# Mask operands in the rounded 32-bit type, and a list scheduler that knows kinds of matmul

## The chip, the core and the metric

The kernel runs on one core of a Trainium2 chip. The metric is device time in microseconds (us) for one execution. The core has five engines that run their own instruction streams: TensorE (PE; its weight loads are shown apart as PEld), VectorE (DVE), ScalarE (ACT), GpSimd (POOL) and SyncE (SP), which here only issues DMAs. They wait for one another through semaphores.

## The reference

Three stages follow one another. The sizes are 4 batches, 768 tokens, 8 heads of 48, model width 384, inner width 1024, 4 experts of 64.

```python
# stage 1, for every batch and head: a complex decay a_t, normalised, and a running state
S_re = ar*S_re - ai*S_im + k_t (x) v_t ;  S_im = ar*S_im + ai*S_re ;  y_t = q_t . S_re
# stage 2: a gated inner layer with a convolution of 3 taps along the tokens
h = relu(x @ w_in);  conv = sum_k conv_w[k] * shift(h, k);  x2 = (h * sigmoid(conv)) @ w_out
# stage 3: attention of 4 experts, each token mixing its best 2
scores = (x2 wq_e)(x2 wk_e)^T / 8, upper triangle set to -1e9;  a = softmax(scores)
out += [e in top 2] * w_e * (a @ (x2 wv_e)) @ wo_e
```

## The kernel before

All three stages are written as one list of operations (`S.op`), each with the engines that may run it, an estimated duration, the tiles it reads and writes, and a priority. `Sched.run` (lines 159 to 314) then plays a machine: at each moment it takes, for the engine that is free first, the ready operation with the smallest priority number that has buffer space, and `emit` writes the instructions in the order so found. The table `P` holds the offsets from which all priorities are made, and the buffer counts. So the order on every engine is fixed when the kernel is built; on the chip each engine works through its own list and waits only for data.

Buffers are arenas: F, R, Z, A to D in SBUF, and the 8 PSUM banks ("banks" in the rows). A matmul operand of the rounded 32-bit type (`F32R`) is made by a copy that rounds, followed by a subtraction that keeps the remainder; products are formed from the high and low parts. These matmuls are called rounded here: L743 and L781 (the two products of stage 2, nine matmuls each time), L901 (queries and keys), L851 (values), L1000 and L1001 (scores), L979 (output). Full 32-bit matmuls are L423, L571, L583, L591, L609, L613 (stage 1), L1024 and L947 (128x128 transposes by a matmul with the identity) and L958 (weights times values). L609, L613 and L958 use 48 or 64 of the 128 columns.

A score operation (`score`, L985) takes one block of 128 queries against n = 128 to 768 keys. It runs L1000 and L1001 over n columns, in two pieces where n is over 512, and then L1003, a matmul of `identb` (weights) with `maskb` (moving) that adds 1e30 above the diagonal of the last 128 columns. Both tiles are BF16. DVE then reduces the row minimum (L1009), ACT takes the exponential (L1011), and the transposes (L1024, in `turn`) turn the result, whose copies out of PSUM are L370 on ACT and L372 on DVE.

Idle gaps of PE in the first microseconds are filled with L627, matmuls of a zero tile.

Of the kernel before, what the change touches and what calls it, by code (L numbers as in the profile page):

```python
# [38 lines left out]
P = dict(tu=22.99, lag=1.78, tf=3.56, dn=29.40, pa=28.16, pf=31.65, pp=31.74, ps=19.16, pr=13.53, kn=9.56, pd=-10.31,  # L39
         py=-3.49, cw=7.07, cs=6.91, ne=3, sw=16.78, slack=0.33, hold=1.18, wl=0.23, bl=0.07, bc=0.37, hy=7.06,  # L40
         tb=28.68, xp=-21.85, jq=-1.43, jp=3.08, jv=-4.00, ja=-2.43, jf=16.61, jt=5.79, ju=0.10, jw=0.26, na=13, no=2,
         nt=6, ns=4, nx=7, nq=14, th=0.46, fr=0.20, nc=2, sd=1, ck=-587.37, up=61.76, big=0, a0=1, a1=4, u0=-0.59,
         u1=0.11, u2=3.11, u3=-0.41, u4=0.75, u5=1.55, u6=-0.26, u7=1.62, u8=0.57, u9=-4.01, u10=-7.57, u11=-0.52,
         v0=-0.57, v1=-0.88, v2=2.18, v3=0.15, v4=1.22, v5=1.18, v6=0.00, v7=-7.38, v8=-7.08, v9=-5.79, v10=3.04,
         v11=-7.00, b0=0.00, b1=-4.24, b2=-0.23, b3=7.87, b4=-0.60, b5=-0.53, b6=-3.32, b7=-1.95, b8=-2.61, c0=0.89,
         c1=-2.69, c2=1.81, c3=-0.52, pw=0.14, sp=1.00, jg=-4.92, pm=-1.39)
# [3 lines left out]
COLS = {"F": 19200, "R": 16420, "Z": 8264, "A": 2080, "B": 2080, "C": 2080, "D": 2080}  # L50
# [44 lines left out]
class Sched:  # L95
# [64 lines left out]
    def run(self):  # L160
        slack = P["slack"]
# [6 lines left out]
        dma, curtab, now, port, narrow = 0.0, None, 0.0, 0.0, 0.0  # L168
# [29 lines left out]
        while done < total:  # L198
# [492 lines left out]
def s2_ops(c):  # L691
# [42 lines left out]
    def ft(w, left, right, f, d, xh, xl, acc, group, nx, no):  # L734
# [62 lines left out]
def s3_ops(c):  # L797
# [21 lines left out]
    def batch(b):  # L819
# [22 lines left out]
        for i in range(NCB):  # L842
            ps = S.bank([128, NE + E], tag="pp", bufs=2)
            xh, xl = x2[i // 3]
            o = (i % 3) * 128

            def f(e, ps=ps, xh=xh, xl=xl, o=o):
                z = 0
                for x, a in ((xh, 0), (xl, 0), (xh, 1)):
# [5 lines left out]
            S.op({"PE": 9 * 0.12}, f, r=[xh, xl, wv[0], wv[1]], w=[ps], prio=pz)
# [35 lines left out]
    def project(n, wt, pr, tt, x, qk, pz):  # L891
# [80 lines left out]
    def final(b, i, o, y, d):  # L972
# [13 lines left out]
    def score(b, pr, i, r, d, qk, rs, at):  # L986
# [257 lines left out]
```

## Time and profile before

| what | us |
|---|---|
| median of 3 runs | 691.02 |
| lowest, highest | 687.9, 691.45 |
| the profiled execution, whole | 693.14 |
| its span in the profile | 691.3 |

The profiled execution took 1.8 us more than its span. Start and duration in a timeline row are us from the span's start. A matmul's shown duration reaches to its last result, so neighbours overlap; what a matmul costs PE is read from start to start. A run of n equal matmuls shows (n-1) spacings and one duration.

### The profile page before, as it was taken

What the parts mean: (1) busy time and instruction counts of PE and PEld (TensorE: products, weight loads), DVE (VectorE), ACT (ScalarE), POOL (GpSimd) and SP (SyncE); (2) the same over time, 40 slices, a digit from 0 to 9 for tenths busy, and PEclk for the clock granted to TensorE, in tenths of its full rate; (3) what the DMA queues carried; (4) which work ended last, traced back from release to release, by engine and by line L of the source; (5) the groups of instructions that cost most, each with busy time, mean ns of one, the idle gap of its engine ahead of it and who ended that gap; (6) DMA issues with size and microseconds to landing.
All of it is one profiled execution on the core that took longest, in us unless ns stands there. A gap on an engine that the chain in (4) does not pass through costs nothing.

```text
span 691.3 us, 13153 instructions
## 1 busy us (share of the span) xinstructions
PE 648.2 (94%) x4774; PEld 577.4 (84%) x4778; DVE 564.1 (82%) x1144; ACT 478.7 (69%) x1003; POOL 113.7 (16%) x157
## 2 busy tenths in 40 slices
PE   6789798899899999999999999989999999999995
PEld 3559587799899899999999999977878789788874
DVE  6998999989899999988759999687867676786661
ACT  7967886788898886875536756477667646766752
POOL 0723120240441411110011000011012100100101
PEclk9997999899999999999999999999999999999998
DMA  8665858746657366445132140020021001000102
GB/s 309 164 201 174 242 165 233 201 147 190 169 175 214 100 214 181 144 127 161 58 92 75 65 127 34 17 86 2 1 57 49 35 1 69 1 1 13 36 24 74
DMA packets 54603, 76.57 MB, mean 111 GB/s; under 512 B 5104, under 2 KB 45936, under 8 KB 54528
## 3 DMA queue, kind: packets, MB, share of 16 engines
q1 hardware_dynamic: 54240, 75.04, 35.7%
q8 instruction: 39, 0.64, 0.4%
q0 software_dynamic: 288, 0.59, 0.3%
q14 instruction: 36, 0.29, 0.1%
HBM read 42.51 MB, written 14.16 MB: 82 GB/s over the span
## 4 chain that ended last, share of the span: by engine, by line
PE 63%; DVE 19%; ACT 8%; DMA 5%; issue 3%; SPq 1%; DVEq 0%; ACTq 0%
PE banks L781 12%; PE banks L743 10%; PE banks L958 6%; PE banks L901 5%; PE banks L1024 4%; PE banks L571 4%; PE banks L851 3%; PE banks L979 3%; DVE arena_F L380 3%; PE banks L1000 3%; PE banks L423 3%; DVE arena_R L380 3%; PE banks L1001 2%; PE banks L591 2%; PE banks L609 2%
## 5 line engine op out<-in xcount | busy, mean ns | idle before, releaser
L781 PE MATMUL banks<-arena_R 128*128 128x384 f32 (+1 forms) x510 | 104.1, 343 | 0.0
L743 PE MATMUL banks<-arena_R 128*128 128x384 f32 (+1 forms) x472 | 101.6, 343 | 2.4 <-DVE arena_Z L596 0.9
L781 PEld LDWEIGHTS banks<-arena_R 128*128 128x128 f32 x510 | 88.3, 188 | 1.7 <-issue 1.3
L370 ACT ACTIVATE arena_F<-banks 128x384 f32<-128x384 f32 (+4 forms) x145 | 61.9, 453 | 39.8 <-PE banks L1024 18.7
L743 PEld LDWEIGHTS banks<-arena_R 128*128 128x128 f32 x472 | 82.3, 188 | 4.6 <-ACT arena_R L370 1.3
L765 DVE SCALAR_TENSOR_TENSOR arena_F<-arena_F 128x386 f32<-128x386 f32 (+1 forms) x128 | 77.5, 626 | 4.2 <-ACT arena_F L762 2.9
L370 ACT ACTIVATE arena_R<-arena_F 128x384 fp32r<-128x384 f32 (+2 forms) x82 | 43.0, 534 | 48.9 <-PE banks L781 20.5
L1011 ACT ACTIVATE arena_F<-banks,arena_F 128x128 f32<-128x128 f32 (+5 forms) x96 | 60.6, 640 | 14.4 <-DVE arena_F L1009 13.1
L380 DVE TENSOR_TENSOR arena_R<-arena_F,arena_R 128x384 fp32r<-128x384 f32 (+1 forms) x88 | 57.3, 668 | 14.6 <-PE banks L781 10.1
L380 POOL TENSOR_TENSOR arena_F<-arena_F 128x768 f32<-128x768 f32 x26 | 50.3, 1941 | 107.9 <-ACT arena_F L458 29.3
L1009 DVE TENSOR_REDUCE arena_F<-banks 128x1 f32<-128x128 f32 (+5 forms) x96 | 57.0, 617 | 8.3 <-PE banks L1003 7.6
L380 DVE TENSOR_TENSOR arena_F<-arena_F 128x768 f32<-128x768 f32 (+1 forms) x65 | 61.0, 954 | 0.5 <-ACT arena_F L437 0.3
L344 ACT ACT_TABLE_LOAD x40 | 51.3, 1283 | 1.4 <-PEq L1236 0.8
L1024 PE MATMUL banks<-ident,arena_F 128*128 128x128 f32 x336 | 49.0, 276 | 0.6 <-ACT arena_F L370 0.4
L754 ACT ACTIVATE arena_F<-banks 128x384 f32<-128x384 f32 (+1 forms) x64 | 31.0, 486 | 25.5 <-PE banks L743 21.7
L1000 PE MATMUL banks<-arena_R 128*128 128x384 f32 (+4 forms) x112 | 41.7, 375 | 1.6 <-ACT arena_F L1011 1.6
L372 DVE COPY arena_F<-banks 128x512 f32<-128x512 f32 (+4 forms) x75 | 37.6, 516 | 6.7 <-PE banks L1024 2.8
L958 PE MATMUL banks<-arena_F 128*64 128x384 f32 (+2 forms) x288 | 41.4, 430 | 0.0
L609 PE MATMUL banks<-arena_Z 128*64 128x128 f32 x384 | 37.5, 283 | 3.9 <-DVE arena_Z L573 3.0
L1024 PEld LDWEIGHTS banks<-ident,arena_F 128*128 128x128 f32 x336 | 37.1, 141 | 3.2 <-ACT arena_F L370 1.3
L768 DVE SCALAR_TENSOR_TENSOR arena_F<-arena_F 128x384 f32<-128x384 f32 (+1 forms) x64 | 36.4, 588 | 3.6 <-ACT arena_F L767 3.2
L573 DVE TENSOR_TENSOR arena_Z<-banks,tri 128x512 f32<-128x512 f32 x48 | 31.9, 681 | 5.9 <-PE banks L571 5.2
(242 smaller groups left out, 1480.0 us busy)
## 6 DMA issues: line engine op xcount, KB each, us to landing
arena_F<-x_scr SPq DMA_DIRECT2D x12, 576.0 KB, 4.5
arena_Z<-v SPq DMA_DIRECT2D x12, 512.0 KB, 5.0
arena_C<-arena_F SPq DMA_DIRECT2D x36, 129.0 KB, 2.4
arena_F<-q SPq DMA_DIRECT2D x12, 384.0 KB, 3.8
arena_F<-k SPq DMA_DIRECT2D x12, 384.0 KB, 4.7
arena_B<-arena_F SPq DMA_DIRECT2D x36, 128.0 KB, 2.4
x_scr<-arena_Z SPq DMA_DIRECT2D x24, 192.0 KB, 3.5
out<-arena_F SPq DMA_DIRECT2D x24, 192.0 KB, 1.9
```

The source lines that it names most:

```text
L344: nc.scalar.preload_act_table_set(TABS[o.tab])
L370: self.A.activation(out(), in_(), AF.Copy)
L380: self.E[e].tensor_tensor(out(), a(), b(), op=self.OPS[op])
L609: PE.matmul(ps[64 * i:64 * i + 64, g_, :], v[:, ci, 2 * g_ + i, :], sm[g_ // 2][:, 2 * (g_ % 2) + i, :], start=True, stop=(cc == 0))
L743: PE.matmul(ps.ap, wi[f][a][:, i * 128:(i + 1) * 128], x[i].ap, start=(n == 0), stop=(n == 8))
L765: S.op({"DVE": dve(no) + 0.06}, lambda e, i=i: V.scalar_tensor_tensor(cv.ap, h[:, i:i + no], cw[:, k3 + i:k3 + i + 1], cv.ap, op0=OP.mult, ...
L781: PE.matmul(o[:, i, :], a[:, m * 128:(m + 1) * 128], g_.ap, start=(f == 0 and n == 0 and len(g) == 1), stop=(f == FT - 1 and n == 2 and i ...
L958: PE.matmul(py[64 * r:64 * r + 64, :n], v[kb][:, o:o + HD], at[r][:, kb, :n], start=(kb == 0), stop=(kb == nk - 1))
L1000: PE.matmul(pp, q[:, qs], k[:, kk], start=True, stop=False)
L1009: S.op({"DVE": dve(n)}, lambda e: V.tensor_reduce(nm.ap, view(), axis=AX.XY, op=OP.min), r=[ps], w=[nm], prio=d)
L1011: S.op({"ACT": act(n) + 0.15}, lambda e: A.activation(a.ap.rearrange("p (x y) -> p x y", x=nb), view(), AF.Exp, bias=nm.ap, scale=-1.0, ac ...
L1024: PE.transpose(pt[:, z, :], a[:, (g_ + z) * 128:(g_ + z + 1) * 128], ident)
```

## The change

Four things change. `identb` and `maskb` become F32R, which takes 128 columns of four bytes off arena Z. Rounded operations are named "r". In the scheduler, a rounded operation that follows one of another kind is charged 0.085 us more, and while the last PE operation was of another kind a rounded one is ranked 3.00 later (`md`). And nearly all numbers of `P` are new. Everything behind line 271 stands 4 lines later in the changed kernel: L1003 becomes L1007, L1024 becomes L1028, L573 becomes L577.

```diff
-P = dict(tu=22.99, lag=1.78, tf=3.56, dn=29.40, pa=28.16, ...
+P = dict(tu=22.99, lag=1.78, tf=3.56, dn=26.46, pa=28.16, ...
...
-         c1=-2.69, c2=1.81, c3=-0.52, pw=0.14, sp=1.00, jg=-4.92, pm=-1.39)
+         c1=-3.06, c2=1.81, c3=-2.94, pw=0.11, sp=2.10, md=3.00, jg=-4.85, pm=-2.48)
-COLS = {"F": 19200, "R": 16420, "Z": 8264, ...
+COLS = {"F": 19200, "R": 16420, "Z": 8136, ...
...
-            cand = [(rank(o, to) if e == "ACT" else o.prio, o.i, o) for o in heaps[e] if o.ready <= now]
+            cand = [(rank(o, to) if e == "ACT" else o.prio + (P["md"] if e == "PE" and o.name == "r" and mode != "r" else 0.0),
+                     o.i, o) for o in heaps[e] if o.ready <= now]
...
             dur = o.alts[e] + (0.015 if e == "PE" else 0.0)
+            if e == "PE":
+                dur += 0.085 if o.name == "r" and mode != "r" else 0.0
+                mode = o.name
...
-        S.op({"PE": pd}, sc, r=need, w=[ps], prio=d)
+        S.op({"PE": pd}, sc, r=need, w=[ps], prio=d, name="r")
...
-    identb = consts.tile([128, 128], BF16, name="identb")
+    identb = consts.tile([128, 128], F32R, name="identb")
     nc.vector.tensor_copy(identb, ident)
-    maskb = consts.tile([128, 128], BF16, name="maskb")
+    maskb = consts.tile([128, 128], F32R, name="maskb")
     nc.vector.tensor_scalar(maskb, jp, 0.0, 1e30, op0=OP.is_gt, op1=OP.mult)
```

The other rounded products (L743, L781, L851, L901, L979) get `name="r"` in the same way.

On PE, in the first batch of stage 3, scores and transposes alternate in the kernel before; `identb` is loaded by a separate instruction.

```order
L1024 MATMUL banks<-ident,arena_F 128x128 x9
L1000 MATMUL banks<-arena_R 128x128
L1001 MATMUL banks<-arena_Z_3301,arena_R 128x128
L1003 LDWEIGHTS identb
L1003 MATMUL banks<-maskb,identb 128x128
L1000 MATMUL banks<-arena_R 128x128
L1001 MATMUL banks<-arena_Z_3301,arena_R 128x128
L1003 LDWEIGHTS identb
L1003 MATMUL banks<-maskb,identb 128x128
```

In the changed kernel the same place on PE reads so (L1004, L1005 and L1007 are the score, L905 is queries and keys, L951 and L1028 are transposes).

```order
L1004 MATMUL banks<-arena_R 128x256
L1005 MATMUL banks<-arena_Z_3284,arena_R 128x256
L1007 MATMUL banks<-maskb,identb 128x128
L905 MATMUL banks<-arena_R,arena_C_3432 128x384 x3
L905 MATMUL banks<-arena_R,arena_D_3462 128x384 x3
L905 MATMUL banks<-arena_R,arena_C_3432 128x384 x3
L951 MATMUL banks<-ident,arena_F 128x128 x3
L1028 MATMUL banks<-ident,arena_F 128x128 x30
```

Scores and projections now stand together, and the transposes that were spread between them come 30 in a row.

On DVE, at the end of stage 1, the last causal products of stage 1 (L573, which PE's last stage-1 matmuls wait for) stand between the subtractions of stage 2 (L380) in the kernel before.

```order
L573 TENSOR_TENSOR arena_Z_113<-banks,tri 128x512
L380 TENSOR_TENSOR arena_R<-arena_F,arena_R 128x384
L372 COPY arena_F<-banks 128x386
L380 TENSOR_TENSOR arena_R<-arena_F,arena_R 128x384
L600 TENSOR_TENSOR arena_Z_113<-banks,arena_Z_113 96x384
L380 TENSOR_TENSOR arena_Z_113<-arena_Z_113,arena_C_436 96x384
L380 TENSOR_TENSOR arena_R<-arena_F,arena_R 128x384 x2
L573 TENSOR_TENSOR arena_Z_113<-banks,tri 128x512
```

In the changed kernel the last two causal products (L577) come as a pair behind the state update (L604, L384) and a step of the convolution (L772).

```order
L604 TENSOR_TENSOR arena_Z_113<-banks,arena_Z_113 96x384
L384 TENSOR_TENSOR arena_Z_113<-arena_Z_113,arena_C_436 96x384
L772 SCALAR_TENSOR_TENSOR arena_F<-arena_F 128x384
L376 COPY arena_F<-banks 128x386 x2
L577 TENSOR_TENSOR arena_Z_113<-banks,tri 128x512 x2
```

The work of stage 1 ends at nearly the same place in DVE's list, and on PE 18 matmuls of L781 (two times nine) that stood ahead of stage 1's end now stand behind it.

## Rows read from the trace of the kernel before

**Rows 1.** The page: engine, busy us (share of the span), instructions.

```profile
PE 648.2 (94%) x4774; PEld 577.4 (84%) x4778; DVE 564.1 (82%) x1144; ACT 478.7 (69%) x1003; POOL 113.7 (16%) x157
```

**Rows 2.** Busy time by stretch: us, then each engine's busy us, PE's clock, DMA.

```profile
200.00:351.00 151.00, 148.33 (x1269) 141.14 (x1270) 134.53 (x231) 111.30 (x204) 27.34 (x39) 1.00 0.48 144
...
450.00:691.00 241.00, 228.62 (x1594) 188.92 (x1594) 164.95 (x395) 147.79 (x390) 21.66 (x26) 0.99 0.09 31
```

**Rows 3.** PE's waits from 450 us on: line, releaser, us, times, longest.

```profile
PE banks L1000 <- ACT arena_F L1011: 1.6, 1, 1.6
PE banks L901 <- DVE arena_R L915: 1.3, 2, 0.8
PE banks L851 <- DVE arena_Z L922: 1.1, 3, 0.8
PE banks L1024 <- ACT arena_F L370: 0.4, 1, 0.4
```

**Rows 4.** PE's timeline: start, us, line. Rounded matmuls behind transposes.

```profile
617.15 0.71 PE L1024 MATMUL banks<-ident,arena_F 128*128 128x128 f32 x5
617.62 1.29 PE L901 MATMUL banks<-arena_B,arena_R 128*128 128x384 f32 x6
618.74 0.51 PE L901 MATMUL banks<-arena_Z,arena_R 128*128 128x384 f32 x2
```

**Rows 5.** The same view, rounded matmuls behind a mask.

```profile
607.31 0.23 PE L1003 MATMUL banks<-maskb,identb 128*128 128x128 bf16 x1
607.35 1.30 PE L901 MATMUL banks<-arena_B,arena_R 128*128 128x384 f32 x6
608.49 0.69 PE L901 MATMUL banks<-arena_Z,arena_R 128*128 128x384 f32 x3
```

**Rows 6.** The same view, scores of 128 columns behind rounded matmuls.

```profile
447.91 0.69 PE L901 MATMUL banks<-arena_Z,arena_C 128*128 128x384 f32 x3
448.43 0.69 PE L901 MATMUL banks<-arena_A,arena_Z 128*128 128x384 f32 x3
448.96 0.22 PE L1000 MATMUL banks<-arena_R 128*128 128x128 f32 x1
449.02 0.28 PE L1001 MATMUL banks<-arena_R 128*128 128x128 f32 x1
449.14 0.23 PE L1003 MATMUL banks<-maskb,identb 128*128 128x128 bf16 x1
...
449.32 0.28 PE L1001 MATMUL banks<-arena_Z,arena_R 128*128 128x128 f32 x1
```

**Rows 7.** The same view, transposes behind a mask, then a score of 128 columns.

```profile
593.32 0.23 PE L1003 MATMUL banks<-maskb,identb 128*128 128x128 bf16 x1
593.38 1.15 PE L1024 MATMUL banks<-ident,arena_F 128*128 128x128 f32 x9
594.29 0.31 PE L1000 MATMUL banks<-arena_R 128*128 128x128 f32 x1
594.44 0.28 PE L1001 MATMUL banks<-arena_Z,arena_R 128*128 128x128 f32 x1
```

**Rows 8.** Weight loads at the place of rows 6.

```profile
448.96 0.19 PEld L1001 LDWEIGHTS banks<-arena_R 128*128 128x128 f32 x1
449.13 0.10 PEld L1003 LDWEIGHTS <-identb 128*128 128x128 bf16 x1
```

**Rows 9.** The mask matmul in the view of tile maskb: ns min/median/max.

```profile
L1003 PE MATMUL banks<-maskb,identb x96: 229/230/235, 449.1 to 668.4; 128*128 128x128 bf16 x96
```

**Rows 10.** PE's timeline: the longest run of transposes and what follows it.

```profile
548.42 2.35 PE L1024 MATMUL banks<-ident,arena_F 128*128 128x128 f32 x20
550.53 0.77 PE L901 MATMUL banks<-arena_Z,arena_R 128*128 128x384 f32 x3
```

**Rows 11.** Timeline of ACT and PE: a run of 11 that waited.

```profile
512.02 1.17 ACT L370 ACTIVATE arena_R<-arena_F 128x1152 fp32r<-128x1152 f32 x1
...
513.17 0.27 PE L1024 MATMUL banks<-ident,arena_F 128*128 128x128 f32 x1
...
513.84 0.33 PE L1024 MATMUL banks<-ident,arena_F 128*128 128x128 f32 x1 [0.39 <-ACT arena_F L370]
...
514.22 0.47 PEld L979 LDWEIGHTS banks<-arena_R 128*128 128x128 f32 x3 [0.24 <-ACT arena_F L370]
```

**Rows 12.** Groups by line and shape: rounding copies on DVE.

```profile
L372 DVE CAST arena_R<-arena_F 128x384 fp32r<-128x384 f32 x16 | 5.6, 352 | 1.4 <-DMA arena_F<-x_scr 1.3
```

More of the change, by code (lines that the diff above doesn't have):

```diff
@@ L38 @@
 TINY64 = 1.125 * 2.0 ** -15
[L39 to L45, printed above, removed]
-         c1=-2.69, c2=1.81, c3=-0.52, pw=0.14, sp=1.00, jg=-4.92, pm=-1.39)
+P = dict(tu=22.99, lag=1.78, tf=3.56, dn=26.46, pa=28.16, pf=31.32, pp=31.74, ps=18.69, pr=13.53, kn=8.85, pd=-10.31,
+         py=-3.16, cw=7.07, cs=6.91, ne=3, sw=19.05, slack=0.33, hold=1.66, wl=0.20, bl=0.07, bc=0.29, hy=7.06,
+         tb=28.32, xp=-19.04, jq=0.16, jp=3.30, jv=-8.28, ja=-3.03, jf=19.36, jt=5.42, ju=0.08, jw=0.27, na=14, no=3,
+         nt=8, ns=4, nx=8, nq=13, th=0.30, fr=0.20, nc=2, sd=1, ck=-653.30, up=61.76, big=0, a0=2, a1=4, u0=-2.43,
+         u1=1.52, u2=3.11, u3=-0.04, u4=0.75, u5=1.00, u6=-0.26, u7=3.93, u8=3.27, u9=-4.01, u10=-7.57, u11=-7.33,
+         v0=-0.57, v1=-2.57, v2=2.62, v3=0.15, v4=1.22, v5=0.95, v6=-4.30, v7=-9.20, v8=-6.49, v9=-1.87, v10=3.04,
+         v11=-4.56, b0=-0.85, b1=-4.25, b2=-0.41, b3=6.82, b4=0.10, b5=-0.53, b6=-2.49, b7=-1.72, b8=-2.19, c0=0.32,
+         c1=-3.06, c2=1.81, c3=-2.94, pw=0.11, sp=2.10, md=3.00, jg=-4.85, pm=-2.48)
 TABS = {"E": "natural_log_exp_and_others", "T": "trig_and_small", "S": "sigmoid_and_others",
@@ L49 @@
 CPY = ("ACT", "DVE", "POOL")
-COLS = {"F": 19200, "R": 16420, "Z": 8264, "A": 2080, "B": 2080, "C": 2080, "D": 2080}
+COLS = {"F": 19200, "R": 16420, "Z": 8136, "A": 2080, "B": 2080, "C": 2080, "D": 2080}
 class Tl:
@@ L167, in run @@
         counts, frees, left, gops = {}, [], {}, {}
-        dma, curtab, now, port, narrow = 0.0, None, 0.0, 0.0, 0.0
+        dma, curtab, now, port, narrow, mode = 0.0, None, 0.0, 0.0, 0.0, ""
         z0 = sum(1 for t in self.tiles if t.left and any(x[-1] == "0" for x in t.regs))
@@ L746, in ft @@
             S.warm = (c.hot[0], S.op({"PE": 0.22}, S.heat, r=xh, w=[c.hot[1]], prio=d), c.hot[1])
-        uo = S.op({"PE": 9 * (max(nx / 2400, 0.107) + 0.0135)}, up, r=xh + xl + list(wi[f]), w=[ps], prio=d)
+        uo = S.op({"PE": 9 * (max(nx / 2400, 0.107) + 0.0135)}, up, r=xh + xl + list(wi[f]), w=[ps], prio=d, name="r")
         if f == 0:
@@ L854, in batch @@
             pz = d + P["jv"] + i
[L855 removed]
+            S.op({"PE": 9 * 0.12}, f, r=[xh, xl, wv[0], wv[1]], w=[ps], prio=pz, name="r")
             c.cp(lambda i=i: v[i].ap, lambda ps=ps: ps[:, :NE], NE, [ps], [v[i]], pz)
@@ L902, in f @@
                     z += 1
-        S.op({"PE": 9 * 0.175}, f, r=[xh, xl, wt[0], wt[1]], w=[ps], prio=pz)
+        S.op({"PE": 9 * 0.175}, f, r=[xh, xl, wt[0], wt[1]], w=[ps], prio=pz, name="r")
         for r in range(2):
@@ L980, in of @@
                     z += 1
-        S.op({"PE": 6 * 0.176}, of, r=[x for p in y for x in p] + [wo[0], wo[1]], w=[po], prio=d)
+        S.op({"PE": 6 * 0.176}, of, r=[x for p in y for x in p] + [wo[0], wo[1]], w=[po], prio=d, name="r")
         t = S.tile([128, DM], tag="o", bufs=3)
```

2 lines of the change are left out of this document (1 added, 1 removed).

## The prediction

> **What bounds the kernel now.** I read the page's busy shares first: PE is busy for 94% of the span, DVE for 82%, ACT for 69% [rows 1]. The reader is to see that no engine but PE is near the span. Then the busy time by stretch: from 200 to 351 us, where stage 1 ends and stage 2 runs beside it, PE is busy 148.3 of 151 us and DVE 134.5; from 450 us on, where stage 3 runs, PE is busy 228.6 of 241 and DVE 165.0 [rows 2]. So from 200 us on PE sets the pace, and an edit is worth what it takes from PE's list. Third, PE's waits: behind 450 us they come to 4.4 us in seven waits [rows 3]. The rest of stage 3 is matmuls, and spacings between them that are longer than the matmul needs. These I read from start to start in PE's timeline.
>
> **The spacings.** Rounded matmuls of 384 columns follow one another every 0.175 us (447.91 to 448.96 is 1.05 for six) and of 128 columns every 0.06 (448.96 to 449.02) [rows 6]. Nine transposes show 1.15 us, which is eight spacings and one duration, 0.28; the spacing is 0.109 [rows 7].
>
> **What a change of kind costs.** The scheduler's new model charges 0.085 us whenever a rounded matmul follows another kind. One place tests it [rows 4]: five transposes start at 617.15, then six rounded matmuls, and the next one starts at 618.74. Spacings alone give 617.15 + 5 x 0.109 + 6 x 0.175 = 618.745. Nothing is lost. (The first rounded one is shown 0.08 early and the second one that much late, which looks like a cost if only that pair is read.) Behind a mask it is otherwise. The mask at 607.31 is followed by the seventh rounded matmul at 608.49 [rows 5]: 1.18 less 1.05 leaves 0.13 for a mask of 128 columns where a rounded matmul of that width takes 0.06. At 449.14 the mask and the L1000 behind it take 0.18 together [rows 6], so 0.12 for the mask, and the L1001 ahead of it takes 0.12 in place of 0.06. With transposes behind it, 593.32 to 594.44 is 1.12, less 9 x 0.109 and 0.06: 0.08 for the mask [rows 7].
>
> **Edit 1, the mask's type.** There are 96 masks [rows 9]. In PE's order of before 48 are followed by a rounded matmul, 43 by transposes, 5 by L958; 16 belong to scores of 128 columns. Their cost now, the five ahead of L958 left out on both sides: 48 x 0.13 + 43 x 0.08 + 16 x 0.06 = 6.2 + 3.4 + 1.0 = 10.6 us. In the changed order 68 are followed by rounded matmuls, 22 by transposes, 6 by L958. A mask between rounded matmuls should cost 0.06. A rounded matmul of 128 columns straight ahead of a transpose is not in the trace: between 0.06 and the 0.12 that a mask takes between two kinds; I take the middle, 0.09. That is 68 x 0.06 + 22 x 0.09 = 4.1 + 2.0 = 6.1. The edit gives back 10.6 - 6.1 = 4.5 us, all on PE, all behind 449 us. If the 0.12 belongs to short matmuls and not to the kind, the new cost is 90 x 0.12 = 10.8 and the gain is nil. If the longer weight load shows, it is a loss, below. DVE's wait for the mask's result grows by about 0.05 us a score (the mask's duration is 230 ns, that of L1001 [rows 6] about 280), which DVE's 76 idle us in this stretch hide; without them it is 96 x 0.05 = 4.8.
>
> **The identity's weight load.** The load of the BF16 identity takes 0.10 us, that of a rounded operand 0.19 [rows 8]. At 448.96 such a load of 0.19 stood ahead of a matmul that began 0.06 behind the last, so loads lie beside earlier matmuls, and I count nothing.
> The Trainium skill, page "TensorE: Matmul & The Clock Gate", section "Weight-path perf modes — Fast Weight Load (FWL) and DoubleRow", says that a fast load reads weights 32 bits at a time and so gains nothing for 32-bit weights. That speaks against this edit, and the two durations agree with it; by the rule, with the load in the open, the sum would be the last rival's.
>
> **Edit 2, the price and the preference in the scheduler.** Rounded runs that start behind transposes or other full matmuls fall from 125 to 91 in PE's order. By the test above [rows 4] each gives back nothing: 0 us. By the model it would be 34 x 0.085 = 2.9, and with the 48 masks counted too 82 x 0.085 = 7.0 us.
>
> **Edit 3, the new order.** Both orders issue the same 3785 matmuls, 96 fillers among them, and the same number of DMAs; up to about 85 us PE's list is the same row for row. Two places move.
> At the end of stage 1, 18 matmuls of L781 come behind it: 18 x 0.175 = 3.1 us. They are moved inside a stretch in which PE is 98% busy [rows 2], so the sum of PE's work is as before and I count nothing. If DVE holds the end of stage 1 instead, PE idles ahead of it and has 3.1 us more to do behind it. DVE's share speaks for some of that: it makes 14 more rounding copies of 384 or 386 columns in the whole program, 14 x 0.35 = 4.9 us [rows 12].
> In stage 3 the transposes come in 39 runs and not 64, and runs of twelve or more rise from 2 to 14. A longer run has more copies to wait for. The run of 20 lost nothing: 548.42 to 550.53 is 2.11 for 20 x 0.109 = 2.18, the next start being shown early [rows 10]. A run of 11 waited because ACT was in a rounding copy of 1.17 us: 513.17 to 513.84 and on to 514.22 is 1.05 for two transposes, 0.83 lost [rows 11]. Bounds for the twelve new long runs are 0 and 12 x 0.83 = 10 us. I take 0, from the longer run, and keep the 10. PE's waits of now [rows 3] may also go: at most 4.4.
> Arena Z's 128 lost columns and the two constants (four more bytes to write each, before 10 us) cost nothing on PE; a tile that no longer fits is already in the order.
>
> **The sum.** 693.1 - 4.5 = 688.6 against the profiled execution. That run is 2.1 above the median of the three, so for a median 691.0 - 4.5 = 686.5 us.
>
> **The rivals.**
> 1. The forecast, 686.5; its own range 681 to 690 (PE's late waits gone [rows 3], or most of the 3.1 of stage 1 paid). Chance 0.47.
> 2. No change, 690 to 692. Either the 0.12 stays for short matmuls, or stage 1's end is held by DVE and its 3.1 eats most of the 4.5. For it: DVE is 89% busy there; against it: 0.06 between rounded matmuls [rows 6]. Chance 0.25.
> 3. Slower: transposes in long runs wait for their copies out of PSUM in stage 3, 0.83 for each of twelve, 10 - 4.5 = +5.5: 696.5. It decides from 4.5 / 12 = 0.38 us a run. For it: the run of 11 [rows 11], and the run of 30 behind many scores whose exponentials keep ACT. Against it: the run of 20 [rows 10], and ACT is busy 148 of 241 us. Chance 0.17.
> 4. Much faster: the model is right and each of the 82 changes saves 0.085: 691.0 - 7.0 = 684. Against it stands that test [rows 4]. Chance 0.08.
> 5. The mask's load is in the open: 0.09 on top of 0.06 for each of 96, 14.4 in place of 10.6, +3.8: 695. Against it stand the loads that are hidden now [rows 6, 8]. Chance 0.03.
>
> **How the numbers follow.** Half a per cent, 3.5 us, is about what a measurement here can tell from none; the three runs themselves spread over that much. Faster is below 687.6, slower above 694.5. Of the forecast some two thirds lie below 687.6 (0.31), all but a little of rival 4 (0.07), and a little of rivals 2 and 3, since a new order can also shorten waits ahead of 200 us (0.06): 0.44. Slower takes most of rival 3 (0.13), rival 5 (0.02) and 0.04 from the others: 0.19. The rest, 0.37, is within. The range of 8 in 10 is 679 to 697: from the forecast with PE's late waits gone [rows 3] and 3 us of the early waits too, up to rival 3.
>
> **What would show it.** L1007 should be shown as a 32-bit matmul, the spacing from a mask to the second rounded matmul of 384 columns should fall from about 0.30 to 0.235, and the L1005 of 128 columns ahead of a mask should be followed in 0.06. The stretch from the first mask to the end should be shorter by 4 to 5 us with PE's waits about as now. If stage 1's last matmul, now at about 351 us, moves by more than 2 us, the step on its end is wrong; if rows of L1028 carry waits on L370 or L372 of more than 4 us in all, rival 3 is at work; if spacings behind transposes shrink, rival 4.

## The result: slower by 1.2%, and the profile after

The changed kernel takes 700.16 us (median of 20 runs, 694.75 to 705.31), the kernel before 691.67 (20 runs) beside it: ratio 1.0116, 95% interval 1.0093 to 1.0139. The forecast was 686.5, the range ended at 697. The profiled execution has a span of 699.1 us (691.3 before). Times here and below are medians of all executions, while the ratios leave out the few that ran slow, so the two can differ by some 0.3%.

The page's busy shares, of after, against [rows 1]: PE has nearly the same busy time (646.7 and 648.2 us), in a longer span.

```profile
PE 646.7 (93%) x4774; PEld 584.9 (84%) x4778; DVE 571.1 (82%) x1153; ACT 479.5 (69%) x1005; POOL 113.8 (16%) x151
```

The busy times from 85 to 200 us (columns as in [rows 2]: PE, PEld, DVE, ACT, POOL), of after:

```profile
85.00:200.00 115.00, 100.56 (x809) 93.62 (x809) 107.73 (x195) 86.79 (x155) 33.16 (x33) 0.97 0.55 163
```

and of before:

```profile
85.00:200.00 115.00, 105.04 (x872) 100.11 (x871) 107.78 (x199) 95.50 (x176) 29.20 (x32) 0.96 0.64 186
```

From 85 to 200 us PE is busy 4.5 us less and runs 63 matmuls fewer; DVE is as busy as it was, 94%. The time goes where the prediction did not look. PE's timeline shows stage 1's last four matmuls and the last group of stage 3's output, first of before, then of after (start, us, line).

```profile
351.26 0.39 PE L613 MATMUL banks<-arena_D,arena_Z 96*48 96x128 f32 x4
...
676.65 6.58 PE L979 MATMUL banks<-arena_R 128*128 128x384 f32 x36
```

```profile
356.42 0.39 PE L617 MATMUL banks<-arena_D,arena_Z 96*48 96x128 f32 x4
...
684.01 6.56 PE L983 MATMUL banks<-arena_R 128*128 128x384 f32 x36
```

Stage 1 ends 5.2 us later, although 3.1 us of stage 2 that stood ahead of its end now stand behind it. From there to the end of the output it is 331.97 us before (676.65 + 6.58 - 351.26) and 334.15 after: 2.2 more. That is less than the 3.1 us that came behind it, so there is no sign that stage 3 itself lost anything. PE's waits from 450 us on, against [rows 3], are twelve of 5.0 us in all; those of the transposes that were to decide rival 3 are small (2.3 us in all, where its sign was 4). The two largest rows:

```profile
PE banks L905 <- DVE arena_R L919: 0.9, 1, 0.9
PE banks L1028 <- ACT arena_F L374: 0.9, 2, 0.5
```

PE's longest single wait in the whole of after is new (line, releaser, us, times, longest):

```profile
PE banks L617 <- POOL arena_F L756: 5.0, 1, 5.0
```

The releaser shown, two columns of zeros, is only what POOL did next. The timelines of POOL, DVE and PE at that place show the cause; L384 on POOL is the state product of chunk 8, which these matmuls read.

```profile
161.44 3.64 POOL L384 TENSOR_TENSOR arena_F<-arena_F 128x768 f32<-128x768 f32 x2 [6.25 <-DVE arena_F L384]
165.03 5.69 POOL L384 TENSOR_TENSOR arena_Z<-arena_Z,arena_B 96x384 f32<-96x384 f32 x1
```

```profile
165.21 2.20 DVE L769 SCALAR_TENSOR_TENSOR arena_F<-arena_F 128x386 f32<-128x386 f32 x4
167.33 0.95 DVE L384 TENSOR_TENSOR arena_F<-arena_F 128x768 f32<-128x768 f32 x1
168.20 0.95 DVE L499 SCALAR_TENSOR_TENSOR arena_F<-arena_F 128x768 f32<-128x768 f32 x1
169.07 0.95 DVE L453 SCALAR_TENSOR_TENSOR arena_F<-arena_F 128x768 f32<-128x768 f32 x1
169.94 0.88 DVE L503 COPY arena_F<-arena_F 128x3 f32<-128x3 f32 x1
```

```profile
170.78 0.67 PE L617 MATMUL banks<-arena_D,arena_Z 96*48 96x128 f32 x4 [5.00 <-POOL arena_F L756]
171.24 0.64 PE L613 MATMUL banks<-arena_Z 128*64 128x128 f32 x4
171.66 0.64 PE L617 MATMUL banks<-arena_D,arena_Z 96*48 96x128 f32 x4
```

A product of this size took 0.84 us on POOL in the kernel before:

```profile
175.73 0.84 POOL L380 TENSOR_TENSOR arena_Z<-arena_Z,arena_A 96x384 f32<-96x384 f32 x1
```

Here it ends only when DVE, which ran seven instructions without a gap, has come to a copy of three columns. That copy takes 0.88 us, and 0.16 at 204 us of the same trace, so it too was held up. Then PE goes on at a lower granted clock, 0.56 from 171 to 178 us: mostly the lower of its two levels (1.2 of 2.4 GHz), behind 6 us in which it was busy for 0.83 (groups of four matmuls 0.43 apart; without the wait they are 0.22 apart, below). The number behind POOL's is the clock:

```profile
165.00:171.00 6.00, 0.83 (x7) 0.42 (x8) 6.00 (x10) 2.11 (x5) 5.80 (x4) 0.94 0.92 272
171.00:178.00 7.00, 7.00 (x48) 6.59 (x47) 1.83 (x4) 2.97 (x5) 0.00 (x0) 0.56 0.75 197
```

The mask against [rows 9, 5]: its type changed, its price hardly did. In PE's timeline of after:

```profile
463.45 0.52 PE L855 MATMUL banks<-arena_R,arena_A 128*128 128x260 f32 x3
463.81 0.34 PE L1004 MATMUL banks<-arena_Z,arena_R 128*128 128x384 f32 x1
...
464.17 0.22 PE L1007 MATMUL banks<-maskb,identb 128*128 128x128 f32 x1
464.23 0.57 PE L855 MATMUL banks<-arena_R,arena_A 128*128 128x260 f32 x3
464.64 0.52 PE L855 MATMUL banks<-arena_R,arena_B 128*128 128x260 f32 x3
```

Three L855 take 0.36 (463.45 to 463.81). From the mask to the second group it is 0.47, so the mask takes 0.11; the row behind it, 0.06 later, is shown early, as rounded matmuls behind transposes are. Before it was 0.13 in the same kind of place [rows 5]. The weight load ahead of it, in the view of tile maskb (ns min/median/max), is the longer one:

```profile
L1007 PEld LDWEIGHTS banks<-maskb,identb x96: 187/188/192, 455.5 to 675.7; 128*128 128x128 f32 x96
L1007 PE MATMUL banks<-maskb,identb x96: 218/223/279, 455.5 to 675.8; 128*128 128x128 f32 x96
```

### The profile page after: what moved, and what is told of

Same layout as the page of the kernel before. It is cut to its first block, busy times and chain, and to the rows that moved or that the text cites. A ratio compares the mean times of both kernels' runs of the same rounds, so it can differ in the third digit from the quotient of the medians.

```text
span 699.1 us, 13186 instructions
## 1 busy us (share of the span) xinstructions
PE 646.7 (93%) x4774; PEld 584.9 (84%) x4778; DVE 571.1 (82%) x1153; ACT 479.5 (69%) x1005; POOL 113.8 (16%) x151
## 4 chain that ended last, share of the span: by engine, by line
PE 59%; DVE 20%; DMA 7%; ACT 6%; issue 5%; POOL 2%; SPq 1%; DVEq 0%; ACTq 0%; POOLq 0%
PE banks L785 11%; PE banks L747 9%; PE banks L962 5%; PE banks L1028 5%; PE banks L575 4%; PE banks L855 4%; PE banks L905 3%; PE banks L983 3%; DVE arena_F L384 3%; PE banks L1004 3%; PE banks L595 2%; PE banks L613 2%; PE banks L1005 2%; DMA x_scr<-arena_Z 2%; PE banks L427 2%
## 5 line engine op out<-in xcount | busy, mean ns | idle before, releaser
L785 PE MATMUL banks<-arena_R 128*128 128x384 f32 (+1 forms) x486 | 98.6, 343 | 0.1
L747 PE MATMUL banks<-arena_R 128*128 128x384 f32 (+1 forms) x432 | 91.2, 347 | 1.3 <-DVE arena_Z L577 0.7
L769 DVE SCALAR_TENSOR_TENSOR arena_F<-arena_F 128x384 f32<-128x384 f32 (+1 forms) x128 | 84.2, 679 | 8.0 <-ACT arena_F L766 4.3
L785 PEld LDWEIGHTS banks<-arena_R 128*128 128x128 f32 x486 | 84.0, 188 | 1.9 <-issue 1.5
L747 PEld LDWEIGHTS banks<-arena_R 128*128 128x128 f32 x432 | 76.6, 192 | 2.8 <-DVE arena_Z L577 1.1
L384 POOL TENSOR_TENSOR arena_F<-arena_F 128x768 f32<-128x768 f32 x26 | 51.8, 1998 | 105.7 <-ACT arena_F L441 21.0
L384 DVE TENSOR_TENSOR arena_R<-arena_F,arena_R 128x384 fp32r<-128x384 f32 (+3 forms) x89 | 57.3, 660 | 10.4 <-PE banks L785 4.3
L384 DVE TENSOR_TENSOR arena_F<-arena_F 128x768 f32<-128x768 f32 (+1 forms) x65 | 58.1, 910 | 7.9 <-ACT arena_F L441 5.1
L374 ACT ACTIVATE arena_R<-arena_F 128x384 fp32r<-128x384 f32 (+4 forms) x62 | 33.5, 554 | 35.4 <-PE banks L785 12.6
L1028 PE MATMUL banks<-ident,arena_F 128*128 128x128 f32 x336 | 45.3, 276 | 2.3 <-ACT arena_F L374 0.9
L771 ACT ACTIVATE arena_F<-arena_F 128x384 f32<-128x384 f32 (+1 forms) x64 | 32.2, 522 | 14.6 <-DVE arena_F L769 14.2
L1028 PEld LDWEIGHTS banks<-ident,arena_F 128*128 128x128 f32 x336 | 36.5, 141 | 5.7 <-issue 1.7
L962 PE MATMUL banks<-arena_F 128*64 128x384 f32 (+2 forms) x288 | 39.8, 420 | 0.3 <-DVE arena_F L384 0.3
L376 DVE COPY arena_F<-banks 128x512 f32<-128x512 f32 (+4 forms) x69 | 34.1, 513 | 4.0 <-PE banks L951 1.0
L577 DVE TENSOR_TENSOR arena_Z<-banks,tri 128x512 f32<-128x512 f32 x48 | 31.8, 679 | 6.3 <-PE banks L575 5.2
L772 DVE SCALAR_TENSOR_TENSOR arena_F<-arena_F 128x384 f32<-128x384 f32 (+1 forms) x64 | 34.3, 552 | 3.0 <-ACT arena_F L771 2.5
```

Source lines behind the costliest of these rows:

```text
L374: self.A.activation(out(), in_(), AF.Copy)
L384: self.E[e].tensor_tensor(out(), a(), b(), op=self.OPS[op])
L747: PE.matmul(ps.ap, wi[f][a][:, i * 128:(i + 1) * 128], x[i].ap, start=(n == 0), stop=(n == 8))
L769: S.op({"DVE": dve(no) + 0.06}, lambda e, i=i: V.scalar_tensor_tensor(cv.ap, h[:, i:i + no], cw[:, k3 + i:k3 + i + 1], cv.ap, op0=OP.mult, ...
L772: S.op({"DVE": dve(no)}, lambda e: V.scalar_tensor_tensor(cv.ap, cv.ap, 1.0, h[:, 1:1 + no], op0=OP.add, op1=OP.mult), r=[(h, (0,))], w=[c ...
L785: PE.matmul(o[:, i, :], a[:, m * 128:(m + 1) * 128], g_.ap, start=(f == 0 and n == 0 and len(g) == 1), stop=(f == FT - 1 and n == 2 and i ...
```

## The experiments

Ratios are to the kernel before, run beside each experiment on the same chip (its medians there lie between 691.37 and 692.86 us), with 95% intervals; "new order" is the changed kernel's. Executions of one kernel spread by some 11 us (686.76 to 698.12 before), and much of that lies ahead of stage 1's end: in e3's profile, with before's order on PE, stage 1's last matmuls start at 355.69 us and not at 351.26, while the stretch behind them is no longer (330.35 us). So single profiles are read for their rows and waits, and not for their end.

**e1, the state product of chunk 8 on DVE, new order.**

```diff
-            o.fn(o.eng)
+            o.fn("DVE" if getattr(o, "name", "") == "st8" else o.eng)
```

> The changed kernel with one instruction moved: the state product of chunk 8 (L384, 96x384), which GpSimd runs in 5.69 us at 165 us and for which TensorE waits 5.0 us and then runs 6.8 us at half clock, is issued on VectorE at the same place of the list; nothing else differs. Theory A (this one product, starved by VectorE, makes most of the loss): 5.0 us of wait and about 3 us of half clock go, VectorE takes 0.55 to 0.8 us more; the time falls by 5 to 8 us, to 692 to 695 us, ratio to the kernel before 1.000 to 1.006. Rival B (the new order as a whole is worse, any wait that goes is taken up by the next one within stage 1): ratio stays at 1.009 to 1.012. Rival C (long runs of transposes in stage 3): no change, 1.011.

693.85 us, 1.0049 (1.0012 to 1.0086), where the changed kernel has 1.0116. Theory A holds. DVE and then PE in e1 at that place:

```profile
165.82 0.75 DVE L384 TENSOR_TENSOR arena_Z<-arena_Z,arena_B 96x384 f32<-96x384 f32 x1
```

```profile
167.10 0.44 PE L613 MATMUL banks<-arena_Z 128*64 128x128 f32 x4 [0.86 <-DVE arena_F L376]
167.37 0.39 PE L617 MATMUL banks<-arena_D,arena_Z 96*48 96x128 f32 x4
167.59 0.39 PE L613 MATMUL banks<-arena_Z 128*64 128x128 f32 x4
```

The wait of 5.0 is 0.86 and the groups are 0.22 apart. One product out of 151 instructions on POOL made 0.67 of the 1.16% by the two ratios. Their intervals do not overlap, so the gain is real, but they leave its size open from about 0.2 to 1.1 (an estimate from the two intervals). In e1's profile the stretch from stage 1's last matmuls to the end of the output is 334.14 us, as long as in after: e1 takes back only what lay ahead of it.

**e2, BF16 masks in the new order; e3, rounded masks in the old one** (e2 puts the two BF16 lines back; in e3 the identity itself is written as F32R, and the line shown is e3's, the reverse of e2's). Both keep every engine's list, but for one constant's copy that e3 does not need.

```diff
-    maskb = consts.tile([128, 128], BF16, name="maskb")
+    maskb = consts.tile([128, 128], F32R, name="maskb")
```

> The changed kernel with identb and maskb in BF16 again; the order of every engine is the same. Theory A (a matmul of 128 columns costs about 0.11 us whatever its type, when another weight load follows): the mask's type is worth about 1 us either way; going by the spacings behind 68 masks (0.112 rounded against 0.123 BF16) the time rises by about 1 us, ratio 1.011 to 1.014. Rival B (the forecast's 0.06 for a rounded mask): it rises by 68 x 0.07 = 4.8 us, ratio 1.018. Rival C (the longer weight load costs): it falls by 4 us, ratio 1.006.

> The kernel before with the masks' operands in the rounded type (the identity itself is made in that type and serves the transposes too); arenas, priorities and the order of every engine are those of before, but for one constant's copy that is gone. Theory A (about 0.11 us per mask whatever its type): 48 x 0.011 + 43 x 0.007 + 16 x 0.004 = 0.9 us less, ratio 0.997 to 1.001. Rival B (the forecast): 4.5 us less, ratio 0.9935. Rival C (weight load in the open): 4 us more, ratio 1.006.

e2: 700.68, 1.014 (1.0091 to 1.0189). e3: 691.79, 0.9998 (0.9963 to 1.0033). In neither order can the mask edit be told from nothing (after, with rounded masks, has 1.0116). e3 refutes the 4.5 us, since 0.9935 lies outside its interval; e2 alone would not, as 1.018 lies inside its own.

**e4, kinds of matmul by themselves**, a block behind the kernel's end (r is a rounded matmul).

```diff
+        for _ in range(8):
+            for _ in range(4):
+                t()
+            for _ in range(4):
+                r(384)
```

> The kernel before with a block of matmuls behind its end that nothing waits for, each pattern on lines of its own: alternations of 4 transposes and 4 rounded matmuls of 384 columns, 32 of each by themselves, rounded matmuls of 128 and 256 columns by themselves, a rounded one of 384 with one of 128 or with a BF16 mask, a transpose with a rounded one of 128 or a mask. Only the spacings count, not the time. Theory A: transposes against rounded matmuls of 384 in alternation cost within 0.01 us per change of what they cost by themselves; rounded matmuls of 128 columns alone are spaced 0.11, not 0.06; a pair of 384 and 128 rounded takes 0.175 + 0.11. Rival (the scheduler's model): each change into rounded costs 0.085. Rival (the forecast): 128 columns spaced 0.06, the pair 0.235.

PE's timeline in the block: the start of eight rounds of four transposes (L1119) and four rounded (L1116); then 97 rounded in a row, which the view puts into one group (49 of 384 columns and 48 of 128); then BF16 masks (L1122) between rounded ones of 384, and 17 masks in a row.

```profile
696.88 0.60 PE L1119 MATMUL bo<-ident,tri 128*128 128x128 f32 x4
697.24 0.95 PE L1116 MATMUL bo<-bx,bw 128*128 128x384 f32 x4
698.03 0.60 PE L1119 MATMUL bo<-ident,tri 128*128 128x128 f32 x4
...
706.00 3.66 PE L1119 MATMUL bo<-ident,tri 128*128 128x128 f32 x32
709.42 14.16 PE L1116 MATMUL bo<-bx,bw 128*128 128x384 f32 x97
723.41 0.23 PE L1122 MATMUL bo<-maskb,identb 128*128 128x128 bf16 x1
723.45 0.42 PE L1116 MATMUL bo<-bx,bw 128*128 128x384 f32 x1
723.71 0.23 PE L1122 MATMUL bo<-maskb,identb 128*128 128x128 bf16 x1
...
733.85 1.11 PE L1122 MATMUL bo<-maskb,identb 128*128 128x128 bf16 x17
734.77 4.08 PE L1116 MATMUL bo<-bx,bw 128*128 128x256 f32 x32
```

Eight rounds take 9.12 us (696.88 to 706.00), 1.14 each; 4 x 0.109 + 4 x 0.175 is 1.136, so a change into rounded costs some 5 ns and not 85. The 97 take 13.99 us; less 49 x 0.175 that leaves 5.4, or 0.113 for a rounded matmul of 128 columns. A BF16 mask beside a rounded one takes 0.30 - 0.175 = 0.125, among its own 0.92 / 17 = 0.054. Beside transposes, in two further patterns of the block, a pair of one transpose and one rounded matmul of 128 takes 0.197 (731.15 - 728.00 for 16) and a pair with a mask 0.172 (733.73 - 731.15 for 15); less 0.107 for the transpose that leaves 0.09 and 0.065. So rounded 128 columns cost 0.11 among rounded matmuls and 0.09 beside transposes, and the 0.06 of the prediction was the early showing of a row.

**e6, the new table alone; e7, the preference alone**, each planned anew (the diff is e6's; e7 is the changed code with the table of before and md = 3.00).

```diff
-         c1=-3.06, c2=1.81, c3=-2.94, pw=0.11, sp=2.10, md=3.00, jg=-4.85, pm=-2.48)
+         c1=-3.06, c2=1.81, c3=-2.94, pw=0.11, sp=2.10, md=0.00, jg=-4.85, pm=-2.48)
...
-                dur += 0.085 if o.name == "r" and mode != "r" else 0.0
+                dur += 0.0 if o.name == "r" and mode != "r" else 0.0
```

> The new table of priorities and the rounded masks, without the preference (md = 0) and without the charge of 0.085 us in the scheduler; it is planned anew, 27 matmuls of stage 2 stand ahead of stage 1's end that stood behind it before (in the changed kernel 18 the other way round), and six state products are on GpSimd, that of chunk 8 among them. Theory A (the loss was made where the preference pushed stage 2's products back and one product met a dense stretch of DVE): ratio 0.997 to 1.004, no wait of PE over 3 us. Rival B (the new table by itself makes the loss): 1.007 or more.

> The old table of priorities with the preference for the present kind (md = 3.00), the charge of 0.085 us and the rounded masks; planned anew. 18 second products of stage 2 stand behind stage 1's end as in the changed kernel, and the state product of chunk 8 is on GpSimd. Theory A (the loss comes from the plan that the preference makes, whatever the table): ratio 1.006 to 1.014. Rival B (the loss is an accident of the table and the moment at which one state product meets DVE): 0.997 to 1.004.

e6: 695.24, 1.0054 (1.0011 to 1.0097). e7, with the table of before: 699.21, 1.0131 (1.0082 to 1.0181), theory A. With either table the preference puts the 18 matmuls of stage 2 behind stage 1's end; without it 27 stand ahead of it that stood behind. In e7's profile no product on POOL took over 3 us, so the preference loses without that accident too, by four executions. PE's longest waits there between 85 us and stage 1's end are two for DMAs (2.9 and 2.4 us), and before has none for a DMA in that stretch; whether they make the loss is not shown. e6 is not settled: behind stage 1 its profile is 3.4 us shorter than before's (328.53 against 331.97), and by the median it is still a little slower, so, if that stretch is as short in its other executions, it loses the gain and more ahead of stage 1's end. Its profile, the fastest of ten executions, does not show where.

**e9 and e10, rounding copies from DVE to ACT**, on top of e1 and of the kernel before.

(The line is e10's; e9 has e1's case ahead of it.)

```diff
+            o.fn("ACT" if getattr(o, "name", "") == "cv" and o.eng == "DVE" and 75 < o.start < 340 else o.eng)
```

> The changed kernel with the state product of chunk 8 on DVE (as in e1) and with 33 rounding copies of 384 or 386 columns, issued between about 75 and 340 us, moved from DVE to ACT at the same places; the order of PE is untouched. In e1 DVE was busy 112.3 of 115 us between 85 and 200 us, PE 103.7. Theory A (with the state product repaired, what remains of the loss is DVE: it sets the pace of stage 1, PE does less work by stage 1's end and has it behind): some 33 x 0.35 = 11.6 us leave DVE, PE is busy over 105 us between 85 and 200 us, stage 1's end comes 2.5 us or more earlier than in e1, and the time is 688 to 691.5 with 691.7 for the kernel before, ratio 0.994 to 0.9995. Rival B (PE's own order holds the end): ratio 1.002 to 1.006 as in e1. Rival C (ACT's list now delays what stands behind the copies): 1.008 or more.

> The kernel before with its rounding copies of DVE of that stretch (some 27) moved to ACT at the same places, PE's order untouched. The kernel before has DVE busy 107.8 and PE 105.0 of 115 us between 85 and 200 us. Theory A (DVE sets the pace between 85 and 200 us in both orders): 1 to 4 us less, 688 to 690.5, ratio 0.994 to 0.998. Rival B (PE sets it in this order): ratio 0.999 to 1.002. Rival C (ACT is late): over 1.003.

The counts written there were too high: 22 and 14 copies moved (DVE's casts in the whole program fall from 47 to 25 and from 32 to 18), 7.7 and 4.9 us at 0.35. e9: 700.82, 1.012 (1.0063 to 1.0178), rival C's range. e10: 693.2, 1.0014 (0.998 to 1.0048), in its rival B's range. PE was busy 146.8 us from 200 to 351 us in e1 and 141.9 in e9. That the copies came later from ACT's list than from DVE's would explain it, but no run shows it; a wait of 2.3 us that e1's profile has at 0.65 is part of it (below, under e14). Neither tells by itself who holds stage 1's end.

**e12 and e14, four products of stage 2 left out ahead of stage 1's end**, in the old order and in e1's.

```diff
+    dn = [o for o in order if getattr(o, "name", "")[:2] == "dn" and o.name not in ("dn0", "dn7")]
+    skip = [o for o in dn if flag and o.start < flag.start][-6:-2]
...
+            if o not in skip:
+                o.fn(o.eng)
```

> The kernel before with the last four second products of stage 2 ahead of stage 1's end (4 times nine L781 matmuls, 36 x 0.175 = 6.3 us of PE's work) left out; every other instruction keeps its place, the result lacks these four terms. Theory A (stage 1's end waits for DVE, ACT and their round trips; what stands in PE's list ahead of it is beside those): stage 1's last matmul comes at most 2 us earlier and the time falls by 0 to 2 us, ratio 0.997 to 1.0. Rival B, the recorded step (PE is 98% busy there and holds the end, so moved work costs the same wherever it stands): 5 to 6.3 us less, ratio 0.991 to 0.993.

> The changed kernel with the state product on DVE (e1) and likewise the last four second products of stage 2 ahead of stage 1's end left out, 6.3 us of PE's work. Theory A: the time of e1 less 0 to 2 us, ratio to the kernel before 1.002 to 1.005. Rival B (in this order PE holds the end): e1's 1.0049 less 0.8 to 0.9%, ratio 0.996 to 0.997.

e12: 692.5, 0.9983 (0.9955 to 1.0012). e14: 698.5, 1.0088 (1.0054 to 1.0122), no faster than e1. In e12 stage 1 ends within 1 us of where it did, with 6.3 us less for PE to do ahead of it:

```profile
351.88 0.39 PE L616 MATMUL banks<-arena_D,arena_Z 96*48 96x128 f32 x4
...
676.50 6.54 PE L982 MATMUL banks<-arena_R 128*128 128x384 f32 x36
```

From 200 to 351 us PE is busy 144.35 us in place of 148.33 [rows 2], and the time does not follow. What was taken off PE comes back as waits for DVE ahead of stage 1's last groups, where before has none:

```profile
336.60 1.56 PE L594 MATMUL banks<-arena_Z 128*96 128x48 f32 x16 [1.18 <-DVE arena_Z L576]
...
348.17 1.16 PE L574 MATMUL banks<-arena_D,arena_C 96*128 96x128 f32 x8 [0.70 <-DVE arena_Z L603]
350.29 0.44 PE L612 MATMUL banks<-arena_Z 128*64 128x128 f32 x4 [0.97 <-DVE arena_Z L576]
```

These are 2.85 us, and from 336 to 343 us PE's granted clock is 0.76, where before has 1.00 at that place. Rival B, the recorded step, falls.

e14 cannot be set beside e1's profile without one more look. At 211 us of after POOL and DVE meet a second time, and here POOL holds DVE up:

```profile
210.98 3.71 POOL L384 TENSOR_TENSOR arena_F<-arena_F 128x768 f32<-128x768 f32 x2 [4.90 <-ACT arena_F L511]
```

```profile
211.29 2.00 DVE L764 TENSOR_SCALAR arena_F<-arena_F 128x384 f32<-128x384 f32 x1
213.32 1.78 DVE L769 SCALAR_TENSOR_TENSOR arena_F<-arena_F 128x384 f32<-128x384 f32 x1
```

In e1's profile the same tensor_scalar starts 0.05 us ahead of POOL's first product and takes 0.42. Behind it stand the causal products (L577) for which PE waits: 2.27 us in after, 2.4 in e2, 2.3 in e9 and 3.15 in e14, but 0.65 in e1. So some 1.6 us of what e1's profile gains on after's is this wait and not the state product; in executions that have the wait, it is a rival for part of what e1 leaves of the loss, and it parts the profiles of e1 and e14. How often each kernel has it is not known from single profiles.

**e17 and e18, 40 instructions less on DVE (a tap of the convolution), 40 less on ACT (its tanh)**, in the kernel before.

```diff
+            if not (getattr(o, "name", "") == "tap2" and 80 < o.start < 345):
+                o.fn(o.eng)
```

> The kernel before with the second tap of the convolution (40 scalar_tensor_tensor of 384 or 386 columns on DVE, 0.61 us each by their duration, some 24 us of DVE's 242 between 85 and 351 us) left out; PE, ACT and GpSimd keep their lists. Theory A (DVE holds the end of stage 1): its last matmul comes 5 us or more earlier, and since PE then has the same work in less time behind no wait, the time falls by 2 to 6 us, ratio 0.991 to 0.997; PE's waits on DVE between 85 and 352 us shrink. Rival B (ACT or the round trips hold it): ratio 0.998 to 1.002.

> The kernel before with the tanh of the convolution (40 in that stretch, 0.52 us each, some 20 us of ACT's 207) left out; the other engines keep their lists. If ACT holds the end of stage 1: ratio 0.991 to 0.997. If DVE or the round trips do: 0.998 to 1.002.

e17: 686.21, 0.9923 (0.9891 to 0.9956). e18: 690.36, 0.9985 (0.995 to 1.002). PE's work is untouched in both. In e17 stage 1 ends at 343.11, 8 us earlier than in before's profile (the profiles with before's order on PE lie between 351.26 and 355.69), and the rest is as long as before (331.99). From 200 to 351 us, which now holds 8 us of what follows stage 1, DVE falls from 134.53 [rows 2] to 119.25 while PE rises to 149.14:

```profile
343.11 0.39 PE L614 MATMUL banks<-arena_D,arena_Z 96*48 96x128 f32 x4
...
669.68 5.42 PE L980 MATMUL banks<-arena_R 128*128 128x384 f32 x30
```

```profile
200.00:351.00 151.00, 149.14 (x1258) 142.95 (x1257) 119.25 (x204) 104.74 (x198) 22.56 (x38) 1.00 0.49 145
```

So DVE holds the end of stage 1 in the old order, and PE, 98% busy, does not: 24 us off DVE bring some 5 us, 20 us off ACT in the same chain bring at most 0.5%, and 6.3 us off PE bring as little. In the new order this was not tried on DVE.

**e11, e13 and e16, POOL beside DVE**, blocks behind the kernel's end: products of 96x384 on POOL beside rows of one sort on DVE. The loop is e13's; each name stands for one sort of instruction, in the order in which POOL's rows are listed below.

```diff
+            for f, n in ((None, 0), (two, 6), (stt, 10), (one, 10), (frm, 8), (mix, 8), (tin, 10)):
+                V.tensor_copy(g, h)
+                for i in range(n):
+                    f(i)
+                for i in range(3):
+                    G.tensor_tensor(g[:96], g[:96], h[:96], op=OP.mult)
```

> The kernel before with a block behind its end: three products of 96x384 on GpSimd, each waiting for the one ahead of it, alone and beside a row of instructions of DVE of one sort without gaps: 6 of 128x768 with two inputs in SBUF (0.95 us each, 5.3 in all), 10 scalar_tensor_tensor of 384 (0.55 each), 10 tensor_scalar of 768, 8 copies of 512 out of PSUM, 8 products of 512 with one input in PSUM, 12 rounding copies of 384. Theory A (GpSimd comes to SBUF only when DVE has no instruction with two inputs in SBUF at hand): alone 0.84 us each; beside the first two sorts the first product ends only with the row (5 us or more), the others behind it; beside copies out of PSUM and products from PSUM 0.84 each. Rival B (they share it in turns): each product takes about 0.84 plus one or two instructions of DVE, 1.8 to 2.7, in all sorts with two inputs in SBUF. Rival C (GpSimd was slow for a reason of its own): 0.84 in every sort.

> The bench of GpSimd again, with rows on DVE in which no instruction writes what another wrote, so that each starts before the one ahead has ended, as they do beside the product of 5.69 us (starts 0.53 apart, 0.61 shown each). In the first bench each waited for the one ahead, with 0.04 us between them, and GpSimd's products got in at each gap: 1.64 us beside products of 128x768. Theory A (GpSimd gets to SBUF only at a break in DVE's row): the first product beside the 6 products of 768 ends only behind the row, 5.5 to 6.5 us; beside the 10 scalar_tensor_tensor of 384, 5 to 6 us; beside copies out of PSUM 0.99 as alone. Rival B (they take turns by instruction): 1.2 to 1.7 again.

> The kernel before with four rows behind its end. On GpSimd each time a product of 128x768 (1.84 us) and then one of 96x384 (0.84 alone); on DVE four copies out of PSUM of 384 columns, during the last of which the second product is due, then four scalar_tensor_tensor of 386, and in rows 1 and 2 three instructions of 768, and four more of 386. Rows 1 and 3 take the scalar from a tile, rows 2 and 4 as a constant. Theory A (a scalar read from SBUF keeps GpSimd out): the product takes over 4 us in rows 1 and 3, and 0.84 to 1.8 in rows 2 and 4. Rival B (any overlapped row keeps it out when it comes during a copy out of PSUM): over 4 us in all four. Rival C (turns): 0.84 to 1.8 in all four, and the 5.69 us stay unexplained.

POOL in e13, three products each: alone; beside two inputs of 768; scalar_tensor_tensor of 384; tensor_scalar of 768 (one input); copies out of PSUM.

```profile
689.01 3.12 POOL L1129 TENSOR_TENSOR bg<-bg,bh 96x384 f32<-96x384 f32 x3 [11.92 <-DVE bp L1114]
692.61 4.97 POOL L1129 TENSOR_TENSOR bg<-bg,bh 96x384 f32<-96x384 f32 x3 [0.47 <-DVE bg L1125]
700.48 3.77 POOL L1129 TENSOR_TENSOR bg<-bg,bh 96x384 f32<-96x384 f32 x3 [2.90 <-DVE bg L1125]
707.83 7.59 POOL L1129 TENSOR_TENSOR bg<-bg,bh 96x384 f32<-96x384 f32 x3 [3.58 <-DVE bg L1125]
715.89 3.13 POOL L1129 TENSOR_TENSOR bg<-bg,bh 96x384 f32<-96x384 f32 x3 [0.47 <-DVE bg L1125]
```

Beside instructions with two inputs they take turns: each product takes 0.62 more at 768 columns ((4.97 - 3.12) / 3) and 0.22 at 384. Beside the overlapped tensor_scalar row they do not: 7.59 - 3.12 is 4.5 us lost, about the length of that row (4.76 us, ten starts 0.47 apart), and the first of the three takes 5.45 of it. e11, whose row had small gaps, showed 3.77 there. In e16, the row of after with its scalars, the product took 1.30, 0.98, 0.98 and 0.98: rival C, the 5.69 us could not be made again. That the product was slow in the changed order is seen twice (5.69 in after, 5.68 in e2), and e1 shows what it cost. That DVE's row kept POOL out is read from the two timelines, in which the product ends as the row does; no bench shows it, and what in the row did so stays open.

## Why the prediction was wrong

The sign was wrong. By its own steps:

1. "A mask between rounded matmuls should cost 0.06", 4.5 us gained: failed. The 0.06 of [rows 6] was one spacing, with a start that is shown early; the prediction had warned of just that at the transposes and not applied it here. Its own rows held a sign: the weight load of that L1001 runs to 449.15 [rows 8], and its matmul is shown from 449.02. A rounded matmul of 128 columns costs 0.11 (e4), against 0.125 for the BF16 mask beside rounded ones; beside transposes it costs 0.09, as the prediction took it, against 0.065. With these the prediction's own counts give 48 x 0.125 + 43 x 0.065 = 8.8 us before and 68 x 0.113 + 22 x 0.09 = 9.7 after, an estimate: no gain, and e3 measures none. Its rival 2 had the right figure ("the 0.12 stays for short matmuls").
2. "At the end of stage 1 ... PE is 98% busy ..., so the sum of PE's work is as before and I count nothing": failed. The busiest engine is not the one that holds the end here. DVE does (e17 against e18), and PE fills with stage 2 what DVE leaves it (e12). So the 18 matmuls put behind the end cost time there. Of their 3.1 us, 2.2 show between stage 1's last matmuls and the end of the output in after and in e1, and 1.75 in e7 (333.72); e6, with 27 matmuls (4.7 us) moved ahead, is 3.4 shorter. That nothing else in the new order of stage 3 adds to these differences is not shown. The sentence with "If DVE holds the end" named the mechanism, and rival 2 gave it a place, but only as something that eats a gain. The sign that it named, a shift of stage 1's end by more than 2 us, is less than what two profiles of one order differ by (e3).
3. "Two places move" and nothing counts between 85 and 200 us: failed, and it was the largest term. A state product on POOL beside a dense stretch of DVE cost 5 us of PE's time and then a stretch at a lower clock; e1 takes back 0.67 of the 1.16% (1.0116 to 1.0049). Behind 80 us no product on POOL takes over 2.61 us in the trace of before, so its size could not be read there; that the order of this stretch was not opened at all is the fault.
4. No price for a change of kind: held. 5 ns by e4; the scheduler's 0.085 has the size of the early showing of one row (0.08 at [rows 4]), and rival 4 falls.
5. Long runs of transposes cost nothing: held, within 1 us. The twelve waits from 450 us on, 5.0 us against 4.4 [rows 3], hold none of the size that rival 3 needed; it falls. The load of the rounded identity takes 188 ns where that of the BF16 one took 0.10 us [rows 8], and stays hidden; rival 5 falls, e2 and e3 agree.

Together: by the two profiles the 7.8 us (699.1 - 691.3) are 5.2 up to stage 1's end, 2.2 from there to the end of the output and 0.4 behind that. The first part is for the most part the product on POOL, shown by e1 (0.67% by the ratios, within wide limits). The second, 0.3%, is put down to the work moved behind stage 1's end; that is argued from e12, e17 and the lengths above, and no run moved only those matmuls back. The rest is not settled, nor what the preference does in e7, without the accident on POOL, nor why e6 is not faster. No complete version beat the kernel before. (The count of 3785 matmuls is not the trace's, which has 4774 on PE in both kernels; nothing in the sum uses it.)

## What to carry to other kernels

Ask which engine holds a stage's end by taking work off each in turn, not by its busy share: the engine at 98% was filling time, the one at 89% held it (e12, e17, e18). A scheduler's price read from one pair of rows should be measured over a long alternation first. And when a plan is refitted, read the whole of every engine's list, since one instruction on a slow engine can cost more than the term that the change was made for.

## What the runs showed of the hardware

- POOL beside DVE: the bench rows above. The Trainium skill, page "SBUF — State Buffer", section "SBUF: two separate sides", says that the two share a pair of ports, which the one that starts first holds for its whole instruction. The bench agrees for instructions with two inputs in SBUF (turns: 0.62 or 0.22 us more for each product) and with PSUM (no effect, 3.13 against 3.12), and so do the rows of DVE at 211 us, which end 0.2 and 0.4 us behind the two products on POOL. But the overlapped tensor_scalar row kept POOL out for ten instructions and not for one.
- Rounded matmuls of 128 columns follow one another in 0.11 us where BF16 ones of 128 take 0.054; of 384 columns in 0.175 (e4).
- Taking 6.3 us of work off the busiest engine made the kernel no faster (e12): 2.85 us came back as waits for DVE, and the granted clock fell to 0.76 behind the first of them.
- The spread from execution to execution goes with PE's granted clock. In the 86 executions of the kernel before that ran beside the experiments its mean runs from 0.970 to 0.988, and a line fitted through them falls by some 5 us for each 0.01 (correlation -0.75). The twenty of after have a mean of 0.981 where these have 0.979, so after's loss does not come from a lower clock as a whole.
